# Holding TensorE to the program's order in the main loop, with each scores unit as one block

## The chip, the cores and the metric

The kernel runs on one core of a Trainium2 chip. The core has a matrix engine (TensorE, PE in the profile), a vector engine (VectorE, DVE), an activation engine (ScalarE, ACT), a general engine (GpSimd, POOL) and one that issues transfers (SyncE, SP). Each works through its own list of instructions in order, and semaphores hold an instruction until what it needs is there. The metric is the device time of one execution in microseconds, the median of several runs; lower is better. A change of about 0.2% (4.6 us here) is the least that can be told from none.

## The reference

Two stages, for 4 batches of 6080 tokens with 256 channels:

```python
qn = q / (np.linalg.norm(q, axis=1, keepdims=True) + 1e-06)   # over the tokens
kn = k / (np.linalg.norm(k, axis=1, keepdims=True) + 1e-06)
s = kn.transpose(0, 2, 1) @ qn / tau                          # [4, 256, 256]
s = s - s.max(-1, keepdims=True)
a = np.exp(s)
a /= a.sum(-1, keepdims=True) + 1e-09
x = (v @ a).astype(np.float32)                                # attention over channels
h = x @ w_in                                                  # [24320, 2048]
g = h * (1.0 / (1.0 + np.exp(-1.702 * h)))
out = (g @ w_out).astype(np.float32)                          # [24320, 256]
```

The weights `w_in` and `w_out` come as float64.

## The kernel before

**Folding and precision.** The kernel never forms `v @ a`. For each batch it multiplies the 256 x 256 attention matrix into `w_in` (`weights`), and the main loop then runs `v` through the folded weights. To keep float32 accuracy with single-pass products, each operand is split into a high part (a cast on ACT, L78) and a low part (a subtraction on VectorE, L79), and three products stand for one: high x high, high x low, low x high.

**The main loop.** The tokens of a batch are cut into 12 chunks (11 of 512 and one of 448), and the 2048 inner columns into 16 blocks of 128. One step is one pair of chunk and block; a batch has 192 steps, the loop 768. A step has two halves:

- `hidden`: six products of 128 x 512 into `ps_h` (L407; three buffers, shared with other uses), then the chain sigmoid on ACT (`g`, L413), product on VectorE (L414), cast on ACT (`gh`, L78), subtraction on VectorE (`gl`, L79).
- `project`: six products (L432) that add `gh` and `gl` of one step to the two output tiles `ps_o`. In the program it stands two steps behind (`DEPTH = 2`): after `hidden(s)` comes `project(s-2)`. Its first product reads `gh`, its second `gl`.

After a chunk's 16 steps two copies take `ps_o` out, one on VectorE (L440), one on ACT (L442), and two transfers store them.

**Side work.** A table says at which step each piece of side work is put into the program. At the second and tenth step of each chunk `v_load` and `v_split` fetch and split the next chunk of v. Every four steps one of 25 units of the next batch's attention is prepared and, three steps later, scored: `prepare` splits q and k (ACT, VectorE), squares them on ACT (L227) and adds the squares up on GpSimd (L229); every second `prepare` starts a load of 512 KB of q and one of k. `score` is, for each of the unit's two 128-token tiles and two halves of the channels, one product of 512 columns (L250: high k against high and low q) and one of 256 (L258: low k against high q), added up in two tiles `s`. The 25th unit is the tail of 64 tokens. Then come the norms (L270 to L304), the softmax (L306 to L335, with a change of ACT's function table to Exp and back to Sigmoid, L325 and L327), the transposes and the new weights. Batch 0 has its weights' conversion from float64 (L110 to L135) among the first steps.

**What sets the order.** The first 60 us (the attention of batch 0) stand under `tc.manual_schedule()`, where every engine runs in program order. From there on a scheduler, which replays the program on a timeline of its own, picks the order of each engine's instructions: a product, a cast or a load may be moved ahead of or behind its place in the program, as long as what it needs is there and its buffer free. So in the kernel before, the six products of a step may stand apart, with products of other steps or of a scores unit between them.

Of the kernel before, what the change touches and what calls it, by code (L numbers as in the profile page):

```python
# [18 lines left out]
P = 128  # L19
# [8 lines left out]
def channel_attention_then_glu(  # L28
# [20 lines left out]
    nc = tc.nc  # L49
    B, N, C = q.shape  # L50
    DFF = w_in.shape[1] // 2
    NC2 = C // P
    NF = DFF // P
    NG = NF // FG
# [8 lines left out]
    NCHUNK = len(chunks)  # L63
# [13 lines left out]
    def split(dst_hi, dst_lo, src):  # L77
        ins = nc.scalar.copy(dst_hi, src)  # L78
        nc.vector.tensor_tensor(dst_lo, src, dst_hi.bitcast(F32), op=ALU.subtract)  # L79
        return ins  # L80
# [85 lines left out]
    class Attention:  # L166
# [65 lines left out]
        def score(self, u, qs, ks):  # L232
            t0, nt, pp = self.units[u]
            if u == 0:
                self.s = [
                    ps_s.tile([P, 2 * C], F32, tag=f"s{i}", name=f"s{i}")
                    for i in range(NC2)
                ]
            for j in range(nt):
                first = u == 0 and j == 0  # L240
                last = u == len(self.units) - 1 and j == nt - 1
                for i in range(NC2):
                    ci = slice(i * P, (i + 1) * P)
                    if self.direct:
                        nc.tensor.matmul(
                            self.s[i][:, :C], lhsT=ks[:, j, ci], rhs=qs[:, j, :],
                            start=first, stop=last,
                        )
                        continue
                    nc.tensor.matmul(  # L250
                        self.s[i],
                        lhsT=ks[:pp, j, 0, ci],
                        rhs=qs[:pp, j, :, :],
                        start=first,
                        stop=False,
                        skip_group_check=True,
                    )
                    nc.tensor.matmul(  # L258
                        self.s[i][:, C:],
                        lhsT=ks[:pp, j, 1, ci],  # L260
                        rhs=qs[:pp, j, 0, :],
                        start=False,
                        stop=last,
                        skip_group_check=True,
                    )

        def norms_a(self):

# [128 lines left out]
    def hidden(at, b, c, f):  # L397
        w = chunks[c][1]
        vh, vl = vtiles[b, c]
        grp, o = divmod(f, FG)  # L400
        fs = slice(o * P, (o + 1) * P)
        wh, wl = at.wh[grp], at.wl[grp]
        ps = ps_h.tile([P, NCH], F32, tag="h", name="ps_h")
        n = 0
        for j in range(NC2):
            for l, r in ((wh, vh), (wh, vl), (wl, vh)):
                nc.tensor.matmul(  # L407
                    ps[:, :w], lhsT=l[:, j, fs], rhs=r[:, j, :w],
                    start=n == 0, stop=n == 3 * NC2 - 1,
                )  # L410
                n += 1
        g = gp.tile([P, NCH], F32, tag="g", name="g")[:, :w]
        newest[0] = nc.scalar.activation(g, ps[:, :w], AF.Sigmoid, scale=1.702)  # L413
        nc.vector.tensor_tensor(g, ps[:, :w], g, op=ALU.mult)  # L414
        gh = gp.tile([P, NCH], F32R, tag="gh", name="gh")
        gl = gp.tile([P, NCH], F32R, tag="gl", name="gl")
        split(gh[:, :w], gl[:, :w], g)
        return gh, gl
# [3 lines left out]
    def project(b, c, f, gh, gl):  # L422
        o, w = chunks[c]
        if f == 0:

            room = [(ps_s, f"s{i}") if (b, c) == (0, 1) else (ps_o, "o") for i in range(NC2)]
            po[b, c] = [p.tile([P, NCH], F32, tag=t, name="ps_o") for p, t in room]
        out = po[b, c]
        for d in range(NC2):
            ds = slice(d * P, (d + 1) * P)  # L430
            for n, (l, r) in enumerate(((wo_h, gh), (wo_h, gl), (wo_l, gh))):
                nc.tensor.matmul(  # L432
                    out[d][:, :w], lhsT=l[:, f, ds], rhs=r[:, :w],
                    start=f == 0 and n == 0, stop=f == NF - 1 and n == 2,
                )
        if f == NF - 1:
            for d in range(NC2):
                osb = op.tile([P, NCH], F32, tag="osb", name="osb")[:, :w]
                if d == 0:
                    nc.vector.tensor_copy(osb, out[d][:, :w])  # L440
                else:
                    nc.scalar.copy(osb, out[d][:, :w])  # L442
                dst = outT[d * P : (d + 1) * P, b * N + o : b * N + o + w]
                nc.sync.dma_start(dst, osb)
# [9 lines left out]
    at = Attention(0, direct=True)  # L454
    nu = len(at.units)
# [53 lines left out]
    start = {}  # L509
# [34 lines left out]

    DEPTH = 2
    late = []
    for b in range(B):
        side = start if b == 0 else {}
        order = [(c, f) for c in range(NCHUNK) for f in range(NF)]
        if b == 0:  # L550
            order[: 2 * NF] = [(c, f) for f in range(NF) for c in range(2)]

        def put(s, fn, *a):
            side.setdefault(s, []).append((fn, a))

        for c in range(2 if b == 0 else 1, NCHUNK + (b + 1 < B)):
            at_v = (c - 1) * NF
            bc = (b, c) if c < NCHUNK else (b + 1, 0)
            if b == 0 and c == 2:
                put(4, v_load, *bc)  # L560
                put(2 * NF - 2, v_split, *bc)
            else:
                put(at_v + 1, v_load, *bc)
                put(at_v + 9, v_split, *bc)
        if b + 1 < B:
            nxt = Attention(b + 1)
            held = {}

            def prep(u, nxt=nxt, held=held):
                held[u] = nxt.prepare(u)  # L570

            def score(u, nxt=nxt, held=held):
                nxt.score(u, *held.pop(u))

            first = 2 * NF + 2 if b == 0 else 20
            for u in range(nu):
                put(first + 4 * u, prep, u)
                put(first + 3 + 4 * u, score, u)
            e = first + 4 + 4 * nu
            put(e, nxt.norms_a)  # L580
            put(e + 4, nxt.norms_b)
            put(e + 9, nxt.norms_c)
            put(e + 10, nxt.softmax_a)
            put(e + 13, nxt.softmax_c)
            put(e + 16, nxt.transposes)
            total = NCHUNK * NF
            at_g = [total - 32, total - 24, total - NF + 5, total - NF + 10]
            assert at_g[0] > e + 18
            for g in range(NG):
                put(at_g[g] - 3, nxt.win_split, g)  # L590
                for i in range(NC2):
                    put(at_g[g] + 2 * i, nxt.weights, g, i)
        for s, (c, f) in enumerate(order):
            gh, gl = hidden(at, b, c, f)
            late.append((b, c, f, gh, gl))
            if len(late) > DEPTH:
                project(*late.pop(0))
            for fn, a in side.get(s, ()):
                fn(*a)
        if b + 1 < B:  # L600
            at = nxt
    while late:
        project(*late.pop(0))


# [25 lines left out]
```

## Time and profile before

| | us |
|---|---|
| median of 3 runs | 2298.78 |
| lowest, highest | 2298.21, 2299.56 |
| the profiled execution | 2298.09 |
| its span in the profile | 2296.3 |
| TensorE busy | 2286.2 |
| VectorE busy | 1374.9 |
| ACT busy | 1224.0 |
| GpSimd busy | 212.3 |

The span runs from the first to the last instruction; the execution's own time has 1.8 us more around it. TensorE is busy for all but 10.1 us of the span. The page's "busy" is the time in which at least one instruction is under way, so an engine with products that follow each other more slowly is still busy: starts of neighbouring products have to be read as well. In the profile's rows a number and "us" come first (start and duration), then engine, line, operation and operands; what stands in square brackets is the idle time before the instruction and what ended it.

### The profile page before, as it was taken

How to read it: one execution, taken by the hardware profiler on the slowest of the kernel's cores; microseconds unless marked ns; L12 is line 12 of the kernel's file. 1: busy time of each engine (PE TensorE's matmuls, PEld its weight loads, DVE VectorE, ACT ScalarE, POOL GpSimd, SP SyncE). 2: the span in 40 equal slices, each digit the busy share in tenths (PEclk: the TensorE clock that was granted, in tenths of full speed). 3: DMA queues.
4: the chain of work that ended last, by engine and by line, in shares of the span. 5: the costliest groups of instructions: out<-in, count | busy, mean ns of one | idle time of the engine just before them, and what ended most of it. 6: DMA issues, size and time to landing. Idle time of an engine off the chain costs nothing.

```text
span 2296.3 us, 27390 instructions
## 1 busy us (share of the span) xinstructions
PE 2286.2 (100%) x10300; PEld 1906.7 (83%) x10300; DVE 1374.9 (60%) x2033; ACT 1224.0 (53%) x2108; POOL 212.3 (9%) x160
## 2 busy tenths in 40 slices
PE   9999999999999999999999999999999999999999
PEld 8878888888888888888888888888888888888888
DVE  7986666565565556565556556656555555555554
ACT  6765555555555555555455555554544444444444
POOL 0022322010020022010002012100000000000000
PEclk9999999999999999999999999999999999999999
DMA  8222111100111121110011111110000000000000
GB/s 309 92 74 74 56 55 61 57 27 19 37 54 56 37 74 56 35 56 18 19 56 46 46 56 56 55 35 28 18 19 28 27 19 28 28 19 28 27 9 18
DMA packets 46389, 109.77 MB, mean 48 GB/s; under 512 B 4528, under 2 KB 8624, under 8 KB 46256
## 3 DMA queue, kind: packets, MB, share of 16 engines
q1 hardware_dynamic: 46256, 108.02, 14.0%
q8 instruction: 80, 1.31, 0.2%
q14 instruction: 53, 0.43, 0.1%
HBM read 83.10 MB, written 24.90 MB: 47 GB/s over the span
## 4 chain that ended last, share of the span: by engine, by line
PE 96%; issue 2%; DVE 1%; ACT 0%; POOL 0%; POOLq 0%; DVEq 0%; ACTq 0%
PE ps_o L432 45%; PE ps_h L407 45%; PE s L250 3%; PE ps_w L372 2%; PE s L258 2%; DVE gl L79 0%; PE ps_x L451 0%; DVE z L127 0%; DVE g L414 0%; PE ps_n L276 0%; PE ps_b L299 0%; POOL rn L284 0%; DVE wl L79 0%; PE ps_t L344 0%; DVE z L121 0%
## 5 line engine op out<-in xcount | busy, mean ns | idle before, releaser
L414 DVE TENSOR_TENSOR g<-ps_h,g 128x512 f32<-128x512 f32 (+1 forms) x768 | 524.0, 683 | 456.9 <-ACT g L413 453.6
L79 DVE TENSOR_TENSOR gl<-g,gh 128x512 fp32r<-128x512 f32 (+1 forms) x768 | 566.1, 739 | 383.2 <-ACT gh L78 379.1
L413 ACT ACTIVATE g<-ps_h 128x512 f32<-128x512 f32 (+1 forms) x768 | 453.6, 592 | 508.4 <-PE ps_h L407 504.4
L78 ACT CAST gh<-g 128x512 fp32r<-128x512 f32 (+1 forms) x768 | 472.0, 615 | 442.7 <-DVE g L414 326.7
L407 PE MATMUL ps_h<-v_h,wh 128*128 128x512 f32 (+1 forms) x1536 | 598.0, 389 | 0.3 <-DVE g L414 0.3
L407 PE MATMUL ps_h<-v_h,wl 128*128 128x512 f32 (+1 forms) x1536 | 596.0, 388 | 1.6 <-DVE wl L79 1.6
L432 PE MATMUL ps_o<-gl,wo_h 128*128 128x512 f32 (+1 forms) x1536 | 596.0, 388 | 1.2 <-DVE gl L79 1.2
L407 PE MATMUL ps_h<-v_l,wh 128*128 128x512 f32 (+1 forms) x1536 | 596.3, 388 | 0.0
L432 PE MATMUL ps_o<-gh,wo_l 128*128 128x512 f32 (+1 forms) x1536 | 595.8, 388 | 0.0
L432 PE MATMUL ps_o<-gh,wo_h 128*128 128x512 f32 (+1 forms) x1536 | 504.2, 389 | 0.0
L407 PEld LDWEIGHTS ps_h<-v_h,wl 128*128 128x128 f32 x1536 | 288.6, 188 | 60.2 <-DVE wl L79 2.5
L407 PEld LDWEIGHTS ps_h<-v_h,wh 128*128 128x128 f32 x1536 | 288.7, 188 | 59.0 <-DVE g L414 1.3
L432 PEld LDWEIGHTS ps_o<-gl,wo_h 128*128 128x128 f32 x1536 | 288.6, 188 | 59.0 <-DVE gl L79 2.4
L432 PEld LDWEIGHTS ps_o<-gh,wo_l 128*128 128x128 f32 x1536 | 288.6, 188 | 57.1
L407 PEld LDWEIGHTS ps_h<-v_l,wh 128*128 128x128 f32 x1536 | 288.7, 188 | 54.2
L432 PEld LDWEIGHTS ps_o<-gh,wo_h 128*128 128x128 f32 x1536 | 286.6, 188 | 56.2 <-ACT win_h L78 0.2
L229 POOL TENSOR_TENSOR acc_q<-acc_q,sq 128x512 f32<-128x512 f32 (+1 forms) x72 | 93.8, 1303 | 1235.2 <-ACT sq L227 1082.8
L229 POOL TENSOR_TENSOR acc_k<-acc_k,sq 128x512 f32<-128x512 f32 (+1 forms) x72 | 112.2, 1558 | 11.1 <-ACT sq L227 10.8
L250 PE MATMUL s<-qs,ks 128*128 128x512 f32 (+1 forms) x288 | 109.1, 395 | 0.0
L258 PE MATMUL s<-qs,ks 128*128 128x256 f32 (+1 forms) x288 | 81.0, 281 | 0.0
L227 ACT ACTIVATE sq<-raw_q 128x512 f32<-128x512 f32 (+1 forms) x96 | 58.2, 606 | 34.0 <-DMA raw_q<-in_q 31.4
L79 DVE TENSOR_TENSOR v_l<-v_raw,v_h 128x1024 fp32r<-128x1024 f32 (+1 forms) x48 | 59.4, 1237 | 11.1 <-ACT v_h L78 10.0
(82 smaller groups left out, 928.0 us busy)
## 6 DMA issues: line engine op xcount, KB each, us to landing
raw_q<-in_q SPq DMA_DIRECT2D x44, 512.0 KB, 4.0
raw_k<-in_k SPq DMA_DIRECT2D x44, 512.0 KB, 4.4
v_raw<-in_vT SPq DMA_DIRECT2D x44, 512.0 KB, 3.8
out_T<-osb SPq DMA_DIRECT2D x88, 256.0 KB, 2.1
words<-in_w_in SPq DMA_DIRECT2D x8, 512.0 KB, 7.5
words<-in_w_out SPq DMA_DIRECT2D x8, 512.0 KB, 3.5
v_raw<-in_vT SPq DMA_DIRECT2D x4, 448.0 KB, 3.6
out_T<-osb SPq DMA_DIRECT2D x8, 224.0 KB, 2.0
```

The lines of the kernel that those rows point to most:

```text
L78: ins = nc.scalar.copy(dst_hi, src)
L79: nc.vector.tensor_tensor(dst_lo, src, dst_hi.bitcast(F32), op=ALU.subtract)
L227: nc.scalar.activation(sq, r, AF.Square)
L229: eng.tensor_tensor(acc, acc, sq, op=ALU.add)
L250: nc.tensor.matmul(self.s[i], lhsT=ks[:pp, j, 0, ci], rhs=qs[:pp, j, :, :], start=first, stop=False, skip_group_check=True,)
L258: nc.tensor.matmul(self.s[i][:, C:], lhsT=ks[:pp, j, 1, ci], rhs=qs[:pp, j, 0, :], start=False, stop=last, skip_group_check=True,)
L372: nc.tensor.matmul(ps, lhsT=l[:, j, ci], rhs=r[:, j, :], start=n == 0, stop=n == 3 * NC2 - 1,)
L407: nc.tensor.matmul(ps[:, :w], lhsT=l[:, j, fs], rhs=r[:, j, :w], start=n == 0, stop=n == 3 * NC2 - 1,)
L413: newest[0] = nc.scalar.activation(g, ps[:, :w], AF.Sigmoid, scale=1.702)
L414: nc.vector.tensor_tensor(g, ps[:, :w], g, op=ALU.mult)
L432: nc.tensor.matmul(out[d][:, :w], lhsT=l[:, f, ds], rhs=r[:, :w], start=f == 0 and n == 0, stop=f == NF - 1 and n == 2,)
```

## The change

Two things change.

1. The whole main loop stands under `tc.manual_schedule(engines={PE})`: TensorE runs its products in the order of the program. The other engines are still ordered by the scheduler, which now has TensorE's order as a given.
2. In `score`, the products of a unit are written as a block: first its four of 512 columns, then its four of 256. Before, each long one was followed by its short one. The unit of attention 0 (`direct`), which has no short ones, keeps its order.

```diff
-            for j in range(nt):
-                first = u == 0 and j == 0
-                last = u == len(self.units) - 1 and j == nt - 1
-                for i in range(NC2):
-                    ci = slice(i * P, (i + 1) * P)
...
+            steps = [(j, i) for j in range(nt) for i in range(NC2)]
...
+            for j, i in steps:
+                nc.tensor.matmul(
+                    self.s[i],
+                    lhsT=ks[:pp, j, 0, i * P : (i + 1) * P],
+                    rhs=qs[:pp, j, :, :],
+                    start=u == 0 and j == 0,
+                    stop=False,
+                    skip_group_check=True,
+                )
+            for j, i in steps:
+                nc.tensor.matmul(
+                    self.s[i][:, C:],
+                    lhsT=ks[:pp, j, 1, i * P : (i + 1) * P],
+                    rhs=qs[:pp, j, 0, :],
+                    start=False,
+                    stop=u == len(self.units) - 1 and j == nt - 1,
+                    skip_group_check=True,
+                )
...
-    for b in range(B):
-        side = start if b == 0 else {}
+
+    with tc.manual_schedule(engines={mybir.EngineType.PE}):
+        for b in range(B):
+            side = start if b == 0 else {}
...
+            for s, (c, f) in enumerate(order):
+                gh, gl = hidden(at, b, c, f)
+                late.append((b, c, f, gh, gl))
+                if len(late) > DEPTH:
+                    project(*late.pop(0))
+                for fn, a in side.get(s, ()):
+                    fn(*a)
...
+        while late:
+            project(*late.pop(0))
```

The body of the loop is only moved in by one level. Line numbers shift by 2 or 3: L407 is now L410, L432 is L435, L250 is L252, L258 is L261, L413 is L416.

**Where the orders differ.** First, TensorE at a scores unit of batch 1. Before (`ps_h` is `hidden`, `ps_o` is `project`, `s_...` are the two score tiles):

```order
L250 MATMUL s_5966<-qs,ks 128x512
L258 MATMUL s_5966<-qs,ks 128x256
L432 MATMUL ps_o<-gh,wo_h 128x512 x2
L250 MATMUL s_5967<-qs,ks 128x512
L258 MATMUL s_5967<-qs,ks 128x256
L250 MATMUL s_5966<-qs,ks 128x512
L258 MATMUL s_5966<-qs,ks 128x256
L250 MATMUL s_5967<-qs,ks 128x512
```

Now:

```order
L435 MATMUL ps_o<-gl,wo_h 128x512
L435 MATMUL ps_o<-gh,wo_l 128x512
L252 MATMUL s_5968<-qs,ks 128x512
L252 MATMUL s_5969<-qs,ks 128x512
L252 MATMUL s_5968<-qs,ks 128x512
L252 MATMUL s_5969<-qs,ks 128x512
L261 MATMUL s_5968<-qs,ks 128x256
L261 MATMUL s_5969<-qs,ks 128x256
L261 MATMUL s_5968<-qs,ks 128x256
L261 MATMUL s_5969<-qs,ks 128x256
L410 MATMUL ps_h<-v_h,wh 128x512
```

The pieces of a unit that lay among the products of several steps are one block between a `project` and the next `hidden`.

Second, ACT at the second step of a chunk (step 273, and alike at steps 225, 241, 257, 305, 417, 433, 449 and 465), where a load of q and k arrives and the last chunk's output is copied out. Before:

```order
L413 ACTIVATE g<-ps_h 128x512
L227 ACTIVATE sq<-raw_q 128x512
L78 CAST gh<-g 128x512
L227 ACTIVATE sq<-raw_k 128x512
L227 ACTIVATE sq<-raw_q 128x512
L227 ACTIVATE sq<-raw_k 128x512
L442 COPY osb<-ps_o 128x512
L413 ACTIVATE g<-ps_h 128x512 x2
```

Now:

```order
L416 ACTIVATE g<-ps_h 128x512
L227 ACTIVATE sq<-raw_q 128x512
L445 COPY osb<-ps_o 128x512
L227 ACTIVATE sq<-raw_k 128x512
L227 ACTIVATE sq<-raw_q 128x512
L227 ACTIVATE sq<-raw_k 128x512
L78 CAST gh<-g 128x512
L416 ACTIVATE g<-ps_h 128x512 x2
```

The cast `gh` moved from behind the first square to behind all four and the copy. On SyncE, which issues the loads, early in batch 1, before:

```order
L199 DMA raw_q<-in_q 128x1024
L199 DMA raw_k<-in_k 128x1024
L386 DMA v_raw<-in_vT 128x2x512
L444 DMA out_T<-osb 128x512 x2
L199 DMA raw_q<-in_q 128x1024
```

Now:

```order
L199 DMA raw_q<-in_q 128x1024
L199 DMA raw_k<-in_k 128x1024
L389 DMA v_raw<-in_vT 128x2x512
L199 DMA raw_q<-in_q 128x1024
L199 DMA raw_k<-in_k 128x1024
L447 DMA out_T<-osb 128x512 x2
```

The second load of q and k in a chunk went from behind the stores to straight behind the load of v; before, that order began two chunks later.

More of the change, by code (lines that the diff above doesn't have):

```diff
@@ L238, in score @@
                 ]
-            for j in range(nt):
-                first = u == 0 and j == 0
-                last = u == len(self.units) - 1 and j == nt - 1
-                for i in range(NC2):
-                    ci = slice(i * P, (i + 1) * P)
[L244 to L256, printed above, removed]
-                    )
[L258 to L265, printed above, removed]
+            steps = [(j, i) for j in range(nt) for i in range(NC2)]
@@ new lines, in score @@
+            if self.direct:
+                for j, i in steps:
+                    nc.tensor.matmul(
+                        self.s[i][:, :C],
+                        lhsT=ks[:, j, i * P : (i + 1) * P],
+                        rhs=qs[:, j, :],
+                        start=u == 0 and j == 0,
+                        stop=u == len(self.units) - 1 and j == nt - 1,
+                    )
+                return
+            for j, i in steps:
[3 more added lines that the diff above has]
+                    rhs=qs[:pp, j, :, :],
+                    start=u == 0 and j == 0,
+                    stop=False,
+                    skip_group_check=True,
+                )
@@ L267, in norms_a @@
+            for j, i in steps:
+                nc.tensor.matmul(
[3 more added lines that the diff above has]
+                    start=False,
+                    stop=u == len(self.units) - 1 and j == nt - 1,
+                    skip_group_check=True,
+                )
         def norms_a(self):
@@ L546, in channel_attention_then_glu @@
     late = []
-    for b in range(B):
-        side = start if b == 0 else {}
[L549 to L601, printed above, removed]
@@ L602, in channel_attention_then_glu, with put, prep, score @@
-    while late:
-        project(*late.pop(0))
+    with tc.manual_schedule(engines={mybir.EngineType.PE}):
+        for b in range(B):
+            side = start if b == 0 else {}
+            order = [(c, f) for c in range(NCHUNK) for f in range(NF)]
+            if b == 0:
+                order[: 2 * NF] = [(c, f) for f in range(NF) for c in range(2)]
+            def put(s, fn, *a):
+                side.setdefault(s, []).append((fn, a))
+            for c in range(2 if b == 0 else 1, NCHUNK + (b + 1 < B)):
+                at_v = (c - 1) * NF
+                bc = (b, c) if c < NCHUNK else (b + 1, 0)
+                if b == 0 and c == 2:
+                    put(4, v_load, *bc)
+                    put(2 * NF - 2, v_split, *bc)
+                else:
+                    put(at_v + 1, v_load, *bc)
+                    put(at_v + 9, v_split, *bc)
+            if b + 1 < B:
+                nxt = Attention(b + 1)
+                held = {}
+                def prep(u, nxt=nxt, held=held):
+                    held[u] = nxt.prepare(u)
+                def score(u, nxt=nxt, held=held):
+                    nxt.score(u, *held.pop(u))
+                first = 2 * NF + 2 if b == 0 else 20
+                for u in range(nu):
+                    put(first + 4 * u, prep, u)
+                    put(first + 3 + 4 * u, score, u)
+                e = first + 4 + 4 * nu
+                put(e, nxt.norms_a)
+                put(e + 4, nxt.norms_b)
+                put(e + 9, nxt.norms_c)
+                put(e + 10, nxt.softmax_a)
+                put(e + 13, nxt.softmax_c)
+                put(e + 16, nxt.transposes)
+                total = NCHUNK * NF
+                at_g = [total - 32, total - 24, total - NF + 5, total - NF + 10]
+                assert at_g[0] > e + 18
+                for g in range(NG):
+                    put(at_g[g] - 3, nxt.win_split, g)
+                    for i in range(NC2):
+                        put(at_g[g] + 2 * i, nxt.weights, g, i)
+            for s, (c, f) in enumerate(order):
[5 more added lines that the diff above has]
+                    fn(*a)
+            if b + 1 < B:
+                at = nxt
+        while late:
+            project(*late.pop(0))
```

## The prediction

> **What bounds the kernel now.** I read the page's engine totals and its chain of waits first, then windows, then the waits of TensorE, then the timeline around the few places where TensorE stands still.
>
> ```profile
> PE 2286.2 (100%) x10300; PEld 1906.7 (83%) x10300; DVE 1374.9 (60%) x2033; ACT 1224.0 (53%) x2108; POOL 212.3 (9%) x160
> PE 96%; issue 2%; DVE 1%; ACT 0%; POOL 0%; POOLq 0%; DVEq 0%; ACTq 0%
> ```
>
> TensorE is the bound: busy 2286.2 us, and 96% of the chain. Windows (us; busy time and count of PE, PEld, DVE, ACT, POOL; clock, DMA share, GB/s) show a full stretch without attention work and the one crowded stretch:
>
> ```profile
> 130.00:140.00 10.00, 7.37 (x30) 4.90 (x29) 10.00 (x15) 4.52 (x9) 3.54 (x3) 1.00 0.01 2
> 1620.00:1900.00 280.00, 280.00 (x1256) 235.46 (x1256) 152.28 (x224) 132.30 (x224) 0.00 (x0) 1.00 0.07 23
> ```
>
> The clock is full (1.00) in both, so it is no term. TensorE's own waits in the main loop are few, and each ends on VectorE:
>
> ```profile
> PE ps_h L407 <- DVE wl L79: 1.6, 2, 1.4
> 132.44 0.19 PEld L432 LDWEIGHTS ps_o<-gl,wo_h 128*128 128x128 f32 x1 [1.67 <-DVE gl L79]
> 132.44 0.50 PE L432 MATMUL ps_o<-gl,wo_h 128*128 128x512 f32 x1 [1.25 <-DVE gl L79]
> 132.78 0.39 PE L432 MATMUL ps_o<-gh,wo_l 128*128 128x512 f32 x1
> ```
>
> So there is little to win: 1.6 and 1.25 us here and 0.3 at 64.79 (below). The change fixes the order of an engine that is nearly always busy; what counts is which results come too late for the fixed order.
>
> **The deadline.** One step, and the side work at a chunk's start:
>
> ```profile
> 877.62 0.38 SPq L386 DMA_DIRECT2D v_raw<-in_vT  x1
> 878.82 0.33 SPq L199 DMA_DIRECT2D raw_q<-in_q  x1
> 879.75 0.39 PE L407 MATMUL ps_h<-v_h,wh 128*128 128x512 f32 x1
> 880.89 0.39 PE L407 MATMUL ps_h<-v_h,wl 128*128 128x512 f32 x1
> 881.37 0.60 ACT L413 ACTIVATE g<-ps_h 128x512 f32<-128x512 f32 x1 [0.73 <-PE ps_h L407]
> 882.00 0.69 DVE L414 TENSOR_TENSOR g<-ps_h,g 128x512 f32<-128x512 f32 x1 [0.63 <-ACT g L413]
> 883.76 0.63 ACT L227 ACTIVATE sq<-raw_q 128x512 f32<-128x512 f32 x1 [1.79 <-DMA raw_q<-in_q]
> 884.29 0.60 ACT L78 CAST gh<-g 128x512 fp32r<-128x512 f32 x1
> 884.53 1.30 POOL L229 TENSOR_TENSOR acc_q<-acc_q,sq 128x512 f32<-128x512 f32 x1 [21.89 <-ACT sq L227]
> 884.93 1.45 DVE L79 TENSOR_TENSOR gl<-g,gh 128x512 fp32r<-128x512 f32 x1 [0.88 <-ACT gh L78]
> 886.59 0.57 ACT L442 COPY osb<-ps_o 128x512 f32<-128x512 f32 x1
> 887.06 0.60 ACT L413 ACTIVATE g<-ps_h 128x512 f32<-128x512 f32 x1
> ```
>
> Six products of one step start 879.75 to 880.89: five intervals, 0.228 us each. Count t from the start of the last one (880.89). In the fixed order 24 products stand behind it before its own project: six of the project two steps back, six of the next hidden, six of the next project, six of the hidden after that. So gh(s) is read by the 25th product after it (t = 25 x 0.228 = 5.70), gl(s) by the 26th (t = 5.93). An undisturbed chain is sigmoid at 0.48, product g at 1.11, gh at 1.80, gl at 2.44, ready at about 3.1: 2.8 us to spare. Before, a late gl cost nothing either, since TensorE was given other products meanwhile.
>
> **Part A, nine chunk starts (steps 225, 241, 257, 273, 305, 417, 433, 449, 465).** The new ACT order puts five operations between a sigmoid and its gh: the square that waits for the load, the copy of the output, three squares. The old order had one. SyncE's order shows why it is nine: there the load of q now always stands straight behind that of v. Before, ACT's wait for it showed at five of them, 1.60, 1.79, 1.19, 1.61 and 2.64 us (mean 1.77), of which first and last:
>
> ```profile
> 834.27 0.63 ACT L227 ACTIVATE sq<-raw_q 128x512 f32<-128x512 f32 x1 [1.60 <-DMA raw_q<-in_q]
> 1451.46 0.63 ACT L227 ACTIVATE sq<-raw_q 128x512 f32<-128x512 f32 x1 [2.64 <-DMA raw_q<-in_q]
> ```
>
> I take the one at 883.76 for all: square at t = 2.87. A square holds ACT 0.53 (883.76 to 884.29), the copy 0.47 (886.59 to 887.06). gh then starts at 2.87 + 4 x 0.53 + 0.47 = 5.46 and its result is taken up 0.64 later (884.29 to 884.93): 6.10, late for 5.70. gl lasts 0.69 alone and took 1.45 beside a GpSimd add; four adds follow these squares, so I take 1.45: ready at 7.55, 1.62 late. Behind a wait the next weights aren't there yet: 132.44 to 132.78 is 0.34, 0.11 above the pitch, and gh and gl wait both: + 0.22. So 1.84 x 9 = **+16.6**. What is late next: behind gh on ACT stands the following sigmoid, due at 12 x 0.228 + 0.48 = 3.22 and run at about 6.0. That uses up its step's 2.8 us of slack and no more, and TensorE's own stand of 1.8 us gives that step room, so I count one loss for each start. The ps_h buffers don't add one: the fourth hidden block ahead needs the delayed product g only at its 43rd product, t = 9.8. With gl at 0.69 it is 1.08 x 9 = 9.7; with loads 1.6 us earlier it is about 0 (a rival); with all as at 1451.46, 0.85 more each, 24.2.
>
> By the Trainium skill, page "TensorE: Matmul & The Clock Gate", section "Step-by-step: what each phase is for", TensorE pulls weight loads ahead of running products, while products keep their order. The load at 132.44, started together with its product, was not ahead of the waiting product; by the rule alone the 0.11 would fall away, 2.0 us less over the nine starts.
>
> By the Trainium skill, page "SBUF — State Buffer", section "Who interferes with whom", a VectorE operation with two SBUF inputs is shut out for the whole of a GpSimd instruction that reads SBUF. The gl at 884.93 would then have run from 885.83 to 886.52; it ended at 886.38, so the trace nearly agrees; by the rule a gl can take up to 1.30 + 0.69 = 1.99, an estimate of 4.9 us more over the nine.
>
> **Part B, softmax, three times.** The new order drops the gh that stood between the exponentials and the second table load.
>
> ```profile
> 512.74 1.28 ACT L325 ACT_TABLE_LOAD   x1
> 515.04 0.60 ACT L78 CAST gh<-g 128x512 fp32r<-128x512 f32 x1
> 515.66 1.28 ACT L327 ACT_TABLE_LOAD   x1
> ```
>
> ACT is away 2.30 + 1.28 = 3.58 us. A sigmoid due as this begins makes gl 3.58 - 2.8 = 0.8 late (0.9 with its reload); one due 0.8 later is on time. Between 0 and 0.9 I take 0.4: **+1.2** (0 to 2.7).
>
> **Part C, norms, in the two batches with GpSimd adds beside them.** VectorE now holds the norms between gl and the next step's g.
>
> ```profile
> 485.95 1.47 POOL L284 TENSOR_TENSOR rn<-rn,half 128x4 f32<-128x4 f32 x1
> 492.68 0.69 DVE L79 TENSOR_TENSOR gl<-g,gh 128x512 fp32r<-128x512 f32 x1 [0.69 <-ACT gh L78]
> ```
>
> From the power to that step's gl 6.73, and 0.69 for it: 7.42. TensorE reads it 31 products after the norms' own (hidden and project in turn, five blocks of six, then gh): 31 x 0.228 = 7.07. Late 0.35 + 0.11 at least; with an add of 1.30 ahead of the power 1.76. I take 0.8: **+1.6** (0 to 3.5).
>
> **Part D, the loop's start.** The first project comes right behind the third hidden block; before, six further blocks came first.
>
> ```profile
> 63.45 0.69 DVE L132 CUSTOM_DVE_ANT_0 win<-z,eighths 128x1024 uint16<-128x1024 uint16 x1
> 64.06 0.68 DVE L414 TENSOR_TENSOR g<-ps_h,g 128x512 f32<-128x512 f32 x1
> 64.10 0.39 PE L407 MATMUL ps_h<-v_h,wl 128*128 128x512 f32 x1
> 64.66 0.42 DVE L121 TENSOR_SCALAR z<-z 128x512 f32<-128x512 f32 x1
> 64.79 0.51 PE L407 MATMUL ps_h<-v_h,wh 128*128 128x512 f32 x1 [0.30 <-DVE g L414]
> ```
>
> The new VectorE order is g, L132, L121, g, gl from 63.45: 0.60 + 0.61 + 0.42 + 0.60 gives gl at 65.68, ready 66.37. It is needed at 64.10 + 2 x 0.228 = 64.56: 1.8 late. Before, TensorE lost 64.79 - 64.33 = 0.46: **+1.4** (0 to 2). The stretch 130 to 140, with VectorE full, loses 1.25 and 1.6 before; the fixed order can lose as much elsewhere in it: **0** (-3 to +3).
>
> **Part E, the score block.** Four 512-column products, then four of 256 columns. Can short ones follow each other at their own pitch?
>
> ```profile
> 308.90 0.28 PE L258 MATMUL s<-qs,ks 128*128 128x256 f32 x1
> 308.90 0.19 PEld L250 LDWEIGHTS s<-qs,ks 128*128 128x128 f32 x1
> 309.01 0.40 PE L250 MATMUL s<-qs,ks 128*128 128x512 f32 x1
> 309.02 0.19 PEld L258 LDWEIGHTS s<-qs,ks 128*128 128x128 f32 x1
> L250 PE MATMUL s<-qs,ks 128*128 128x512 f32 x282 | 106.5, 394 | 0.0
> L250 PE MATMUL s<-qs,ks 64*128 64x512 f32 x6 | 2.6, 444 | 0.0
> ```
>
> A short one holds TensorE 0.11 and two loads start 0.12 apart: **0**. Were the load's 0.19 the floor, 213 pairs of short ones cost 0.075 each, 16 us (a rival). The 64-row unit's products, now in one block, had 50 ns extra in six long ones, 0.3 us; the short ones and those behind each switch taken alike: **-1.2** (-1.2 to 0).
>
> Sum: 16.6 + 1.2 + 1.6 + 1.4 - 1.2 = +19.6 on the profiled execution's 2298.1 (0.7 under the median of 2298.8): 2317.7. I say **2317**.
>
> **Rivals.** Under 0.2% (4.6 us) is about what a measurement of this kernel can't tell from no change.
>
> 1. *Nothing is late any more* (faster). The 2.8 us of slack swallows every disturbance and the old waits go: 1.6 + 1.25 + 0.46, their four reloads (0.44), the switches (1.2): -5.0, 2293. For it: the slack, and VectorE and ACT at 60% and 53%. Against: five operations and a load's wait on ACT are 4 us in one place. It decides if squares start before t = 1.25.
> 2. *The loads come earlier* (same). With the new order of loads, q lands 1.6 us sooner and part A is near 0; B to E remain: +3.0, 2301. For it: ACT's wait was absent at four of the nine starts. Against: q was issued 1.2 us behind v (877.62, 878.82), and the order now puts it there each time.
> 3. *Every start as bad as 1451.46*: 24.2 in place of 16.6, 2325.
> 4. *Short products wait for their weights*: +16, 2333. Against: loads 0.12 apart.
>
> That the order isn't held is no rival: TensorE's listing shows six hidden, six project products and whole score blocks throughout.
>
> **How the numbers follow.** Forecast 0.62 (its own range 2307 to 2323: A from 9.7, the crowded stretch ±3), rival 1 0.08, rival 2 0.16, rival 3 0.09, rival 4 0.05. Faster 0.08, same 0.16 (rival 2), slower 0.62 + 0.09 + 0.05 = 0.76. The range 2300 to 2325 takes in rivals 2 and 3.
>
> **What would show it.** In the new profile: TensorE's waits for gh and gl at project, some 20 to 25 us in all, in nine groups of 1.5 to 2 us each, at chunk starts 49.5 us apart (834.27 to 883.76): near 736, 785, 834, 884 and 982, and 1303, 1352, 1401 and 1451 us, each later by what was lost ahead of it; there, ACT waiting over 1 us for q ahead of a gh. One or two waits by the norms, two before 70 us. Short products at 0.11 between starts. No waits at the chunk starts would make A and the forecast wrong; short ones at 0.19 would make E wrong.

## The result, and the profile after

| | before | after |
|---|---|---|
| median | 2298.49 us (4 runs, 2297.7 to 2299.56) | 2325.6 us (4 runs, 2324.27 to 2327.91) |
| ratio to before, 95% interval | | 1.012 (1.0108 to 1.0132) |
| the profiled execution | 2298.09 us | 2324.27 us |
| its span | 2296.3 us | 2322.5 us |

The changed kernel is slower by 27 us; the prediction had 2317 with a range up to 2325. The sums below are made on the spans: 2322.5 - 2296.3 = 26.2 us.

First the engine totals of the page after, and its chain of waits (shares of the span by engine).

```profile
PE 2292.4 (99%) x10300; PEld 1907.8 (82%) x10300; DVE 1389.6 (60%) x2033; ACT 1246.1 (54%) x2108; POOL 209.6 (9%) x160
PE 88%; DVE 4%; issue 3%; ACT 3%; DMA 2%; POOL 0%; ACTq 0%; SPq 0%; POOLq 0%; DVEq 0%
```

TensorE's share of the chain fell from 96% to 88%, DVE's rose from 1% to 4% and ACT's from 0% to 3%: the chain now goes at times through the operations that make `gh` and `gl`. Which products wait for them is in TensorE's waits (us in all, times, longest):

```profile
PE ps_o L435 <- DVE gl L79: 16.5, 18, 3.1
PE ps_o L435 <- ACT gh L78: 7.0, 10, 1.2
PE ps_h L410 <- DVE wl L79: 0.2, 1, 0.2
```

23.5 us of waiting for `gl` and `gh`, where before one wait of 1.2 us stood. The 1.6 us for `wl` fell to 0.2. Now the start of the chunk at step 273, in the timeline:

```profile
894.82 0.63 ACT L227 ACTIVATE sq<-raw_q 128x512 f32<-128x512 f32 x1 [1.63 <-DMA raw_q<-in_q]
895.36 0.57 ACT L445 COPY osb<-ps_o 128x512 f32<-128x512 f32 x1
896.08 0.63 ACT L227 ACTIVATE sq<-raw_k 128x512 f32<-128x512 f32 x1
896.61 0.62 ACT L227 ACTIVATE sq<-raw_q 128x512 f32<-128x512 f32 x1
897.13 0.61 ACT L227 ACTIVATE sq<-raw_k 128x512 f32<-128x512 f32 x1
897.65 0.60 ACT L78 CAST gh<-g 128x512 fp32r<-128x512 f32 x1
898.29 1.63 DVE L79 TENSOR_TENSOR gl<-g,gh 128x512 fp32r<-128x512 f32 x1 [3.78 <-ACT gh L78]
897.55 0.39 PE L410 MATMUL ps_h<-v_h,wl 128*128 128x512 f32 x1
898.31 0.50 PE L435 MATMUL ps_o<-gh,wo_h 128*128 128x512 f32 x1 [0.37 <-ACT gh L78]
899.97 0.50 PE L435 MATMUL ps_o<-gl,wo_h 128*128 128x512 f32 x1 [1.16 <-DVE gl L79]
900.31 0.40 PE L435 MATMUL ps_o<-gh,wo_l 128*128 128x512 f32 x1
```

ACT waits 1.63 us for q, then works through the square, the copy and three squares before it casts. `gh` is there at 898.29; `gl` takes 1.63 us beside a GpSimd add. Products start at 897.55, 898.31, 899.97 and 900.31: intervals of 0.76, 1.66 and 0.34 us where 0.227 each is usual, so this start costs 0.53 + 1.43 + 0.11 = 2.08 us.

In the same way (interval between product starts less the usual one) all nine starts give 2.0, 1.85, 2.36, 2.08, 0.41, 2.75, 2.2, 1.55 and 2.48 us, 17.7 in all. They rise in the main with ACT's wait for q: 0.83 us at the cheapest, 2.30 at the dearest, of which these are the squares of q:

```profile
995.14 0.63 ACT L227 ACTIVATE sq<-raw_q 128x512 f32<-128x512 f32 x1 [0.83 <-DMA raw_q<-in_q]
1318.91 0.63 ACT L227 ACTIVATE sq<-raw_q 128x512 f32<-128x512 f32 x1 [2.30 <-DMA raw_q<-in_q]
```

The next largest place is the crowded stretch of batch 0, from 119 us on, in the timelines of GpSimd, VectorE and TensorE:

```profile
119.47 1.66 POOL L229 TENSOR_TENSOR acc_k<-acc_k,sq 128x512 f32<-128x512 f32 x1 [7.61 <-ACT sq L227]
121.09 1.73 POOL L229 TENSOR_TENSOR acc_q<-acc_q,sq 128x512 f32<-128x512 f32 x1
119.92 1.76 DVE L127 SCALAR_TENSOR_TENSOR z<-words,z 128x512 uint32<-128x512 uint32 x1
121.72 1.66 DVE L132 CUSTOM_DVE_ANT_0 z<-z,eighths 128x1024 uint16<-128x1024 uint16 x1
123.90 1.16 DVE L79 TENSOR_TENSOR gl<-g,gh 128x512 fp32r<-128x512 f32 x1
121.48 0.50 PE L435 MATMUL ps_o<-gh,wo_h 128*128 128x512 f32 x1 [1.15 <-ACT gh L78]
125.11 0.79 PE L435 MATMUL ps_o<-gl,wo_h 128*128 128x512 f32 x1 [3.13 <-DVE gl L79]
125.71 0.63 PE L435 MATMUL ps_o<-gh,wo_l 128*128 128x512 f32 x1
129.97 0.47 PE L435 MATMUL ps_o<-gh,wo_h 128*128 128x512 f32 x1
```

VectorE's L127 takes 1.76 us here and 0.68 elsewhere, L132 1.66 and 0.68, and the `gl` that waits behind them is 3.13 us late. From 125.71 to 129.97 ten products start 0.426 us apart: half the usual pace. The whole stretch loses 8.3 us (2.0 of it by the pace), against 3.7 in the kernel before.

A third place is the norms, here those of batch 0's loop, in the timelines of VectorE and TensorE:

```profile
492.03 2.30 DVE L295 TENSOR_SCALAR diag<-ident,rn 128x128 f32<-128x128 f32 x2
495.44 0.68 DVE L417 TENSOR_TENSOR g<-ps_h,g 128x512 f32<-128x512 f32 x1
496.82 0.50 PE L435 MATMUL ps_o<-gh,wo_h 128*128 128x512 f32 x1 [1.04 <-ACT gh L78]
```

TensorE waits 1.04 us for a `gh` that is late because VectorE's g is. Four GpSimd adds run from 490.47 to 495.49; beside them the norms' operations hold VectorE until 495.44, and 1.8 us are lost, there and in one further batch.

The sum over the trace, after less before: nine starts +17.7; behind the dearest start, products at half the pace, +1.4; crowded stretch 8.3 - 3.7 = +4.7; norms 2 x 1.8 = +3.6; softmax 3 x 0.74 = +2.2; the tail unit's loads, in two batches, +1.8; the loop's start 1.5 - 0.58 = +0.9; the span's end +0.2: 32.5. Against it stand gains of some 6 us: 1.2 at the tail unit's changes between 64 and 128 rows, about 4 in small delays (below 0.13 us) of products in the main loop and the scores, and some 0.7 outside the loop, most of it where TensorE waits 1.0 us for a load of k instead of 1.7 (1.0 to 2.9 us in these kernels' traces, so that is scatter). 32.5 - 6 = 26.5, for 26.2 measured.

### The profile page after: what moved, and what is told of

It is laid out like the page before. It is cut to its first block, busy times and chain, and to the rows that moved or that the text cites. A ratio compares the mean times of both kernels' runs of the same rounds, so it can differ in the third digit from the quotient of the medians.

```text
span 2322.5 us, 27315 instructions
## 1 busy us (share of the span) xinstructions
PE 2292.4 (99%) x10300; PEld 1907.8 (82%) x10300; DVE 1389.6 (60%) x2033; ACT 1246.1 (54%) x2108; POOL 209.6 (9%) x160
## 4 chain that ended last, share of the span: by engine, by line
PE 88%; DVE 4%; issue 3%; ACT 3%; DMA 2%; POOL 0%; ACTq 0%; SPq 0%; POOLq 0%; DVEq 0%
PE ps_o L435 41%; PE ps_h L410 41%; PE s L252 3%; DMA raw_k<-in_k 2%; PE ps_w L375 2%; DVE gl L79 1%; PE s L261 1%; ACT sq L227 1%; ACT gh L78 1%; DVE g L417 0%; DVE v_l L79 0%; ACT g L416 0%; DMA raw_q<-in_q 0%; ACT v_h L78 0%; PE ps_x L454 0%
## 5 line engine op out<-in xcount | busy, mean ns | idle before, releaser
L416 ACT ACTIVATE g<-ps_h 128x512 f32<-128x512 f32 (+1 forms) x768 | 453.6, 592 | 428.5 <-PE ps_h L410 427.1
L435 PE MATMUL ps_o<-gl,wo_h 128*128 128x512 f32 (+1 forms) x1536 | 597.7, 389 | 16.7 <-DVE gl L79 16.5
L435 PE MATMUL ps_o<-gh,wo_h 128*128 128x512 f32 (+1 forms) x1536 | 596.8, 389 | 7.1 <-ACT gh L78 7.0
L410 PE MATMUL ps_h<-v_h,wh 128*128 128x512 f32 (+1 forms) x1536 | 597.2, 389 | 0.0
L410 PE MATMUL ps_h<-v_l,wh 128*128 128x512 f32 (+1 forms) x1536 | 596.0, 388 | 0.0
L410 PE MATMUL ps_h<-v_h,wl 128*128 128x512 f32 (+1 forms) x1536 | 595.4, 388 | 0.2 <-DVE wl L79 0.2
L435 PE MATMUL ps_o<-gh,wo_l 128*128 128x512 f32 (+1 forms) x1536 | 595.4, 388 | 0.0
L435 PEld LDWEIGHTS ps_o<-gl,wo_h 128*128 128x128 f32 x1536 | 288.5, 188 | 80.1 <-DVE gl L79 23.7
L435 PEld LDWEIGHTS ps_o<-gh,wo_h 128*128 128x128 f32 x1536 | 288.6, 188 | 69.9 <-ACT gh L78 13.2
L410 PEld LDWEIGHTS ps_h<-v_h,wl 128*128 128x128 f32 x1536 | 288.6, 188 | 58.7 <-DVE wl L79 1.0
L435 PEld LDWEIGHTS ps_o<-gh,wo_l 128*128 128x128 f32 x1536 | 288.8, 188 | 56.3
L410 PEld LDWEIGHTS ps_h<-v_h,wh 128*128 128x128 f32 x1536 | 289.0, 188 | 55.1
L410 PEld LDWEIGHTS ps_h<-v_l,wh 128*128 128x128 f32 x1536 | 289.0, 188 | 54.5
L252 PE MATMUL s<-qs,ks 128*128 128x512 f32 (+1 forms) x288 | 78.7, 394 | 0.0
L79 DVE TENSOR_TENSOR qs<-raw_q,qs 128x512 fp32r<-128x512 f32 (+2 forms) x75 | 50.1, 668 | 28.8 <-ACT qs L78 28.6
L78 ACT CAST qs<-raw_q 128x512 fp32r<-128x512 f32 (+2 forms) x75 | 45.3, 604 | 40.9 <-PE s L261 40.4
```

Of the source, the lines that this page charges most:

```text
L252: nc.tensor.matmul(self.s[i], lhsT=ks[:pp, j, 0, i * P : (i + 1) * P], rhs=qs[:pp, j, :, :], start=u == 0 and j == 0, stop=False, skip_gro ...
L410: nc.tensor.matmul(ps[:, :w], lhsT=l[:, j, fs], rhs=r[:, j, :w], start=n == 0, stop=n == 3 * NC2 - 1,)
L435: nc.tensor.matmul(out[d][:, :w], lhsT=l[:, f, ds], rhs=r[:, :w], start=f == 0 and n == 0, stop=f == NF - 1 and n == 2,)
```

## The experiments

Below, "the rule" stands for one edit: the squares that feed GpSimd's adds are queued on ACT directly behind the newest `gh`, so they can't get ahead of it. Ratios are to the kernel before, run on the same chip, with a 95% interval. The opening takes 0.2% as the least that can be told from none; these intervals are 0.09 to 0.17% to either side, so a smaller change is called one here where its interval doesn't reach 1.

### The two halves of the change apart

With the order held, but each long product followed by its short one, as before:

```diff
-            for j, i in steps:
-                nc.tensor.matmul(
-                    self.s[i],
...
-            for j, i in steps:
-                nc.tensor.matmul(
-                    self.s[i][:, C:],
...
+            for j in range(nt):
...
+                for i in range(NC2):
...
+                    nc.tensor.matmul(
+                        self.s[i],
...
+                    nc.tensor.matmul(
+                        self.s[i][:, C:],
...
```

> The change without its second part: TensorE in program order, but each scores unit as before (long product, then its short one). Theory (the loss comes from results that are late for the fixed order): the order is the whole loss, so 2322 to 2330 us, waits of TensorE for gh and gl at project of 20 to 26 us in all. Rival (short products one behind another are the loss): the loss shrinks to half or less, 2312 us or below.

Measured: 2325.18 us (2323.33 to 2331.36), ratio 1.0115 (1.0098 to 1.0132). TensorE's waits (of an execution that took 2331.36 us, the longest of its runs):

```profile
PE ps_o L432 <- DVE gl L79: 17.8, 19, 3.1
PE ps_o L432 <- ACT gh L78: 7.6, 11, 1.3
```

And the scores as a block, without the order:

```diff
-    with tc.manual_schedule(engines={mybir.EngineType.PE}):
-        for b in range(B):
+    for b in range(B):
```

> The second part alone: each scores unit written as four long products and then four short ones, but TensorE's order left to the scheduler. Theory: within 4 us of the kernel before, 2294 to 2302 us, with no wait over 2 us for gh or gl. Rival (the block is the loss): above 2308 us.

Measured: 2294.38 us (2293.99 to 2295.86), ratio 0.9984 (0.9975 to 0.9993).

```profile
PE ps_h L410 <- DVE wl L79: 1.6, 2, 1.4
PE ps_o L435 <- DVE gl L79: 1.2, 1, 1.2
```

The order alone gives the whole loss and much the same waits; the block alone leaves the old waits as they were and wins 3.8 us. The two don't simply add: with the order held the block moved the median by 0.4 us, less than the runs scatter.

### What makes the starts late: the load, or the queue on ACT

The first try was to let q be issued ahead of v:

```diff
-                    put(at_v + 1, v_load, *bc)
+                    put(at_v + 5, v_load, *bc)
```

> The changed kernel with the load of v four steps later in the table (fifth step behind, sixth step of a chunk instead of its second), so that at a chunk's start the load of q and k isn't behind it. Theory (a late q holds ACT, and gh stands behind it): the waits at the nine chunk starts (17.7 us by the trace, and 2 us at a lower clock behind one of them) fall to 3 us or less, 2304 to 2310 us. Rival (ACT's five operations are too long even with the data there): waits of over 1 us stay at the nine starts, 2318 us or above.

Measured: 2324.92 us (2324.07 to 2328.57), ratio 1.012 (1.0105 to 1.0135). SyncE's and ACT's rows at one start:

```profile
787.11 0.38 SPq L389 DMA_DIRECT2D v_raw<-in_vT  x1
788.35 0.33 SPq L199 DMA_DIRECT2D raw_q<-in_q  x1
793.96 0.63 ACT L227 ACTIVATE sq<-raw_q 128x512 f32<-128x512 f32 x1 [2.22 <-DMA raw_q<-in_q]
```

The load of v still stands 1.24 us ahead of that of q: the edit didn't move what it was meant to move, and the run says nothing on its question.

The second try gives the chain more time instead: from step 48 on, `project` stands three steps behind, so that `gh` and `gl` are read 12 products (2.7 us) later. Every fourth step's `gh` and `gl` lie in buffers that are idle by then.

```diff
+    DEEP = 48
...
-        gh = gp.tile([P, NCH], F32R, tag="gh", name="gh")
+        step = b * NCHUNK * NF + c * NF + f
+        spare = step >= DEEP and step % 4 == 3
+        gh = (cv if spare else gp).tile([P, NCH], F32R, tag="z" if spare else "gh", name="gh")
...
-                if len(late) > DEPTH:
+                if len(late) > (3 if b * NCHUNK * NF + s >= DEEP else 2):
```

> The changed kernel with project three steps behind hidden instead of two, from step 48 on (a fourth buffer for gh and gl out of the pool of the finished weight conversion). That gives every gh and gl twelve more products, 2.7 us. Theory (pure lateness against a fixed deadline): the waits at the chunk starts, the norms and the softmax go, those before step 48 stay: 2296 to 2303 us. Rival (ACT or VectorE can't keep up in these places, lateness piles up): over half of the loss stays, 2312 us or above.

Measured: 2298.76 us (2297.75 to 2301.32), ratio 1.0004 (0.9994 to 1.0013).

```profile
PE ps_o L438 <- DVE gl L79: 4.8, 3, 3.1
PE ps_o L438 <- ACT gh L78: 1.2, 1, 1.2
```

The waits that are left lie ahead of step 48, in the crowded stretch and at the loop's start. 26.8 us went. The starts, the pace behind one, norms, softmax and tail loads, as summed above, are 17.7 + 1.4 + 3.6 + 2.2 + 1.8 = 26.7: each of these is a result that is late by less than 2.7 us.

The third leaves the slack alone and clears the queue: the rule.

```diff
-                    nc.scalar.activation(sq, r, AF.Square)
+                    if self.direct:
+                        nc.scalar.activation(sq, r, AF.Square)
+                    else:
+                        with tc.issue_after(newest["gh"].ins):
+                            nc.scalar.activation(sq, r, AF.Square)
...
-        split(gh[:, :w], gl[:, :w], g)
+        newest["gh"] = split(gh[:, :w], gl[:, :w], g)
```

> The changed kernel with one rule for ACT: a unit's squares are queued behind the cast gh of the step in which they stand. Loads, deadline and amount of work stay. Theory (gh behind the squares and the load they wait for is the loss at the nine chunk starts): those waits, 17.7 us and 2 us at a lower clock, go, as the next sigmoid's lateness fits into the slack of 2.8 us; norms, softmax and the stretch near 125 us stay: 2302 to 2309 us. Rival (the lateness only moves on to the next step's sigmoid and its gh): 2316 us or above.

Measured: 2291.59 us (2291.39 to 2293.43), ratio 0.9971 (0.996 to 0.9983), below the expected band. The waits, and the window of the crowded stretch (us; busy time and count of PE, PEld, DVE, ACT, POOL; clock, DMA share, GB/s), of this kernel:

```profile
PE ps_o L439 <- DVE gl L79: 1.6, 4, 0.9
```

```profile
120.00:140.00 20.00, 20.00 (x89) 16.30 (x88) 18.87 (x35) 14.67 (x26) 0.00 (x0) 1.00 0.27 79
```

The same window of the changed kernel:

```profile
120.00:140.00 20.00, 14.82 (x53) 11.09 (x52) 19.19 (x24) 13.21 (x25) 10.54 (x7) 0.83 0.23 79
```

The band had left the crowded stretch as it was. But squares that may not run early bring no adds early: GpSimd is busy 0.00 us there instead of 10.54, VectorE gets 35 operations done instead of 24, TensorE starts 89 products instead of 53, and the clock is full. So the rule took the losses of the stretch and of the norms away together with those of the starts. It moves the squares on ACT and the adds on GpSimd at once; that it is the adds that hold VectorE up rests on the times of L127 and L132 beside them, shown above. And as no run moved the load of q by itself, how much of a start's loss is the late load and how much the operations queued behind it stays open.

### More slack from the first step on

`project` three steps behind from the start of the loop, with the additional `gh` and `gl` in spare weight buffers for the first 64 steps:

```diff
-    DEPTH = 2
+    DEPTH = 3
...
```

> Project three steps behind hidden from the first step on (the fourth buffer for gh and gl lies in an idle weight buffer at first, later in the conversion's pool). Theory (lateness against a deadline, 2.7 us more slack everywhere): beside what the three steps brought from step 48 on, the start's 1.4 us goes and of the 8.8 us near 121 to 132 us some 6, the lower clock among them: 2289 to 2295 us. Rival (VectorE is full there, so more slack only postpones the same wait): 2296 us or above.

Measured: 2295.8 us (2294.91 to 2298.6), ratio 0.9987 (0.9978 to 0.9996).

```profile
PE ps_o L444 <- DVE gl L79: 3.1, 1, 3.1
```

The same with four steps:

```diff
-    DEPTH = 2
+    DEPTH = 4
...
```

> The same with four steps (five buffers). Theory: what is left near 125 us goes too, 1 to 2 us below three steps, 2288 to 2293 us. Rival (a full VectorE sets the rate there): the same time as with three steps, or longer.

Measured: 2300.3 us (2298.22 to 2302.15), ratio 1.0006 (0.9997 to 1.0015).

```profile
PE ps_w L375 <- DVE g L418: 3.3, 1, 3.3
```

With three steps one wait of 3.1 us stays in the crowded stretch; with four, none for `gh` or `gl` stays, but the products of the new weights (`ps_w`) wait for VectorE in their place. The crowded stretch, with three steps:

```profile
120.00:140.00 20.00, 16.94 (x62) 13.38 (x61) 19.93 (x27) 13.22 (x26) 9.62 (x7) 0.83 0.17 56
```

VectorE is full there (19.93 of 20 us) with GpSimd's adds beside it, and slack for one reader only passes the wait on to the next. The stretch still loses 6.2 us of 8.3, where some 6 were expected to go: 2295.8 lies between the two bands, and the trace sides with the rival. With four steps the rival came true.

Three steps with the scheduler free to order TensorE:

```diff
-    with tc.manual_schedule(engines={mybir.EngineType.PE}):
+    if True:
```

> Three steps from the first step on and the scores block, but TensorE's order left to the scheduler. Theory (the free order already fills TensorE, so slack is worth little to it): within 3 us of the scores block alone, 2291 to 2296 us. Rival (the depth itself is the gain, whoever orders): at or below the time of three steps in the program's order.

Measured: 2292.57 us (2291.99 to 2293.67), ratio 0.9974 (0.9964 to 0.9984): below the same with the order held (2295.8). Both of its bands hold this time, so it doesn't tell theory and rival apart. At this distance, too, holding the order wins nothing. The medians differ by 3.2 us; in the traces the stretch loses 6.2 us with the order held, part of it at half the pace (clock 0.83), and 3.8 with it free, where `gl` is waited for once, 1.2 us, as before.

### The rule with the other parts

The rule and three steps from step 48 (both edits above):

> The changed kernel with the squares behind gh, and project three steps behind hidden from step 48 on. Theory: the three waits at the softmax that the squares' rule left (0.74 us each) go too, 2288 to 2291 us. Rival (the longer distance brings waits for the output's copies at chunk ends, as in the run with three steps throughout, 1.4 us): the same as the rule alone, 2291 to 2293 us.

Measured: **2289.14 us** (2288.88 to 2290.99), ratio 0.9962 (0.9949 to 0.9976), the lowest median of all.

```profile
PE ps_o L442 <- DVE gl L79: 0.9, 1, 0.9
```

That is its only wait for `gl`. Against the rule alone 2.45 us are gone; the three softmax losses of 0.74 are 2.2.

The rule with the scores as a block and the order free:

> The scores block and the squares behind gh, with TensorE's order left to the scheduler. Theory (the rule also keeps GpSimd's adds out of the stretch from 120 to 140 us, where the free order loses 3.4 us too): 2289 to 2293 us. Rival (the rule helps only an order that can't step aside): as the block alone, 2294 us or above.

Measured: 2290.74 us (2290.42 to 2291.62), ratio 0.9968 (0.9956 to 0.9981). With the order held it was 2291.59 (2291.39 to 2293.43): ranges that overlap. Once the squares are out of the way, the held order is worth nothing that these runs can tell. Whether the rule, three steps and a free order together would be as fast as 2289.14 wasn't run.

The rule only for the attention that is prepared in batch 0, where the crowded stretch lies, so that the nine starts (steps 225 to 465) stay:

```diff
+                    if self.b != 1:
+                        nc.scalar.activation(sq, r, AF.Square)
+                    else:
+                        with tc.issue_after(newest["gh"].ins):
+                            nc.scalar.activation(sq, r, AF.Square)
```

> The changed kernel with the squares behind gh for the attention of batch 1 alone (prepared during batch 0). The nine chunk starts belong to the attentions of batches 2 and 3 and stay as they were. Theory: the 8.8 us near 121 to 132 us go, the waits at the nine starts stay: 2314 to 2319 us. Rival (the rule works mostly at the chunk starts): 2321 us or above.

Measured: 2317.21 us (2315.76 to 2317.95), ratio 1.0082 (1.0068 to 1.0095). Its waits, and two of its windows, the crowded stretch and the start at step 273:

```profile
PE ps_o L439 <- DVE gl L79: 12.8, 17, 1.2
PE ps_o L439 <- ACT gh L78: 6.4, 10, 1.4
```

```profile
120.00:140.00 20.00, 20.00 (x89) 16.35 (x88) 18.19 (x32) 13.92 (x24) 0.00 (x0) 1.00 0.21 67
892.00:900.00 8.00, 6.86 (x25) 5.54 (x25) 5.25 (x8) 3.58 (x7) 2.44 (x2) 0.79 0.00 0
```

8.4 us went, the stretch's 8.3 and little else. The norms lose 1.8 us in both batches, as without the rule: the adds beside those of batch 0 (482.69 to 487.72) belong to the next attention, whose squares this run leaves free. The half pace now stands behind the start at 892 (1.7 us, clock 0.79 in 8 us) instead of that at 1322 (1.4). The other 25.6 us, down to the rule everywhere, are in this trace the starts, both norms, the tail unit's loads and the pace behind one start: 18.4 + 3.6 + 1.8 + 1.7 = 25.5.

Last the rule in the kernel before, with nothing of the change:

> The kernel before with the squares behind gh and nothing else. Theory: its 3.4 us of waits from 130 to 140 us go, 2293 to 2296 us. Rival (these waits come from VectorE's conversions alone, not from GpSimd's adds): within 1 us of the kernel before.

Measured: 2294.48 us (2293.68 to 2295.2), ratio 0.9983 (0.9975 to 0.9992). The window of the crowded stretch, in the kernel before and then with the rule in it:

```profile
120.00:140.00 20.00, 17.36 (x73) 12.99 (x72) 20.00 (x26) 13.19 (x25) 11.94 (x7) 1.00 0.23 79
```

```profile
120.00:140.00 20.00, 20.00 (x89) 16.49 (x88) 18.73 (x33) 12.67 (x24) 0.00 (x0) 1.00 0.23 79
```

3.85 us went, for the 3.7 that the kernel before loses in its crowded stretch. The early squares hurt it there too; a free order on TensorE hid over half of the harm (3.7 us lost instead of 8.3).

## Why the prediction was right or wrong

**The sign and the mechanism held.** The held order makes results late that nothing waited for before. The order alone gives the loss; slack of 12 products takes 26.8 us of it away; moving the squares behind `gh` takes it all away. Three ways lead to the same cause.

**Part A** was 16.6 and measured 17.7, and all nine starts came where the deadline put them. The start that was used for the sum (883.76, wait 1.79) was a middling one: 1.84 predicted, 1.97 the mean, 0.41 to 2.75 the ends. "One loss for each start" was right for the waits; the product rate behind them was not thought of (below).

**The stretch 130 to 140, "0 (-3 to +3)", is the step that failed.** It measured +4.7, over the whole of 119 to 132. The prediction saw VectorE full and took the loss to be the same under any order of TensorE. What it left out is that a free TensorE took other products while `gl` was late, and that VectorE gets so little done there (24 or 26 operations in the window, 32 to 35 without) because early squares bring GpSimd's adds beside it: without those adds TensorE loses nothing in that window (53 to 89 products with the order held, 73 to 89 with it free). With GpSimd's column of the window (11.94 busy of 20 us) beside VectorE's, that could have been read off the profile of before.

By the Trainium skill, page "SBUF — State Buffer", section "Who interferes with whom", a VectorE operation with two SBUF inputs and a GpSimd operation that reads SBUF shut each other out for a whole instruction. The L127 that began at 119.92 beside the add that ended at 121.13 took 1.76, which is 1.21 of rest of that add and 0.55 for itself (0.68 elsewhere), so the trace nearly agrees, and the prediction, which used that rule for `gl` alone, could have used it here.

**"The clock is full (1.00) in both, so it is no term" failed as well.** It was read off the trace of before, where no wait of the main loop is longer than 1.4 us. After, 2.0 us in the stretch and 1.4 behind the start at 1322 are products at half the pace.

**The norms (1.6 predicted, 3.6 measured) and the softmax (1.2, 2.2)** were right in place and too low, the softmax inside the bounds given for it (0 to 2.7), the norms just above theirs (0 to 3.5). In the norms several operations, not the power alone, ran beside adds: the two `diag` took 2.30 us. The loop's start was 0.9 for 1.4. **The tail unit's loads**, +1.8, had no term: there, too, `gh` stands on ACT behind four squares and the copy. The `gl` behind it (947.22) took 2.57 us beside three GpSimd operations of 0.73 that follow each other, more than the 1.99 that the prediction gave as the most: a `gl` can be held up by several such operations, not by one alone.

**Part E** was right for what it named: the tail unit's changes cost 2.1 us before and 0.9 after, -1.2 as predicted. About 4 us more came back in small delays, for which it had no term. Short products follow each other without a floor, as the row of four and the next product show (302.71 to 303.19 is 0.48 for four, 0.12 each):

```profile
302.71 0.64 PE L261 MATMUL s<-qs,ks 128*128 128x256 f32 x4
303.19 0.40 PE L410 MATMUL ps_h<-v_h,wh 128*128 128x512 f32 x1
```

So rival 4 (the weights' load as a floor, +16) is out. Of the gain, some 3 us are main-loop products that start 0.23 to 0.245 us apart instead of 0.227: what such intervals have above 0.227 adds up to 6.1 us before, 3.6 with the block alone, 3.1 with the order alone and 2.9 after, so either half of the change brings most of it; the tail unit's 1.2 came with the order alone (0.9), not with the block alone (2.1). Why the intervals are longer wasn't tested.

Rivals 1 (nothing late) and 2 (loads earlier) are out by the waits. Rival 3 gave 2325, nearly the time measured, for a wrong reason: all starts dear. They were not; the rest came from the stretch, the norms, the tail and the clock. In sum, the terms that the prediction had came to 17.7 + 2.2 + 3.6 + 0.9 = 24.4 for 20.8, those it had set to nothing or not listed to 4.7 + 1.4 + 1.8 + 0.2 = 8.1, and some 4 us came back in small delays that no term named.

## What to carry to other kernels

When the order of a busy in-order engine is fixed, write down for each result by which product it is read, and look for every place where side work gets into the chain's queues on the other engines; either give that distance (12 products took away 26.8 us here) or queue the side work behind the chain's own operation (34 us, and 3.85 in the kernel before). Look past the queue as well: an early square on ACT brought an early add on GpSimd, and that slowed VectorE, on which the square itself never ran. Together both edits beat the kernel before, 2289.14 against 2298.33 us. Holding the order doesn't seem to be what won it: under the rule alone the held and the free order can't be told apart, though with three steps as well only the held one was run.

## What was not expected of the hardware

After some waits of TensorE products started at half the usual pace, for 2 to 5.5 us. Behind the start at 1322, in the timeline and the window of the changed kernel:

```profile
1322.42 0.50 PE L435 MATMUL ps_o<-gh,wo_h 128*128 128x512 f32 x1 [1.06 <-ACT gh L78]
1324.07 0.50 PE L435 MATMUL ps_o<-gl,wo_h 128*128 128x512 f32 x1 [1.14 <-DVE gl L79]
1324.92 0.63 PE L435 MATMUL ps_o<-gl,wo_h 128*128 128x512 f32 x1
1325.35 0.63 PE L435 MATMUL ps_o<-gh,wo_l 128*128 128x512 f32 x1
```

```profile
1322.00:1330.00 8.00, 6.43 (x22) 5.05 (x23) 4.96 (x7) 3.77 (x8) 3.17 (x3) 0.79 0.00 0
```

Two waits of 1.06 and 1.14 us, with one product between them, and from 1324.92 products start 0.43 us apart. The same happened after 1.15 + 3.13 us (121 to 125), and in other kernels behind other starts (at 892 in the one whose window is shown above, at 750 with the order alone, after 0.43 + 1.16), but not at 1477, whose two waits were 0.78 and 1.15, nor after the single waits of the kernel before (1.25 us at 132.44). A longer wait was enough by itself: 3.06 us with three steps from the first step on, and with the order alone this one, 3.5 us behind an earlier slow spell:

```profile
132.92 0.79 PE L432 MATMUL ps_o<-gl,wo_h 128*128 128x512 f32 x1 [1.88 <-DVE gl L79]
```

So waits of 1.5 us and less did it only where two came close together, and the sum of the two doesn't decide: which of the nine starts is followed by a slow spell changed from kernel to kernel. What decides it stays open.

By the Trainium skill, page "TensorE: Matmul & The Clock Gate", section "Part 1: The HAM clock gate (the "warmup" mystery)", the clock goes to half after an idle window of about 3.4 us that runs freely of the kernel. The half pace agrees with that (0.426 us between starts for 0.227), and a window that runs by itself would fit that the starts differ. A window without any product doesn't fit here: one ran between the two waits at 1322, and 1.88 us is well below 3.4.
